# Mixing the first batch once in full width, and wide mixes for the last six pairs, in a Sinkhorn attention and feed-forward kernel

## The chip, the cores and the metric

The kernel runs on one core of a Trainium2 chip. The metric is the device time of one execution in microseconds (us), as the median over repeated runs. The profiler's span is some 1.8 us shorter than the device time. In profiles, PE is TensorE, DVE is VectorE, ACT is ScalarE, POOL is GpSimd, and SP is the engine that issues stores and transposes here. PSUM is the memory in which products land; the kernel takes it in banks of 512 float columns.

Runs of one kernel shift by about 0.5 us (the kernel before, in its first six runs: 245.0 to 245.1 and 245.6).

## The reference, cut to what matters

```
P = exp(sort_net), rows and columns normalised, five times    # (batch, head, 8, 8)
k_sorted = einsum('bhij,bhjcd->bhicd', P, k_blocks)           # 8 blocks of 96 tokens are mixed
v_sorted = einsum('bhij,bhjcd->bhicd', P, v_blocks)
attn     = softmax(scale * q_block @ k_sorted_block.T)        # within each block
x        = (attn @ v_sorted_block), heads side by side        # (3072, 512)
out      = (x @ w_a * (x @ w_b)) @ w_out                      # feed-forward
```

There are 4 batches of 8 heads. The kernel works on pairs of heads: 16 pairs, numbered 0 to 15, four to a batch. "Mix" below means the product with P.

## The kernel before: the parts that count

TensorE (PE) runs one long instruction stream. A batch's feed-forward products (`pf`, `po`) form the bulk, and the next batch's attention units are set between them: `c` (mix), `s` (scores, exp), `o` (weighted sum, then x). The first batch's attention has nothing to hide behind. Its first four blocks (h=0) are done at the start, the other four (h=1) between the first feed-forward products. So its mixes are halved:

```python
def half_mix(h, hp, what, eng, fill=0, cols=512):
    mix = psF.tile([P, 512], FP32, tag="F", name="mixh")      # one bank, four buffers
    keep_busy(mix, fill, cols)                                # filler products
    for c in range(NCH):                                      # 6
        for e in range(2):
            nc.tensor.matmul(..., lhsT=src2[:, e, c*D:(c+1)*D],
                             rhs=s_all[:, 2*hp + e, h*NBH:(h+1)*NBH], ...)   # 64 columns
    copy(eng, ...)                                            # 384 columns
# later pairs
def stage_mix(g, what, engines):
    mix = psA.tile([P, 2, 512], FP32, tag="A", name="mix")    # two banks, two buffers
    for c in range(NCH):
        for e in range(2):                                    # 12 products, half the array wide
            nc.tensor.matmul(mix[e*D:(e+1)*D, c // 3, c % 3 * P:(c % 3 + 1) * P],
                             lhsT=src2[:, e, c*D:(c+1)*D], rhs=s_all[:, 2*g + e], ...)
    ...                                                       # copies to kT or vT
# ... the scores and o_ps use psA too:
sc = psA.tile([P, 2, 512], FP32, tag="A", name="sc")
```

The softmax here doesn't subtract the row's maximum and nothing guards it: scores larger than these inputs give would overflow.

## Time and profile before

The time was 245.06 us at first and 245.04 us beside the changed kernel. PE's stream is the bound, so I cut it at three marks: the column products of P (`pc_ps`), the first feed-forward product after which PE runs without long gaps, and the first query turn of the second batch (`q_ps`). A fourth mark is where the last batch's `pf` begins. I call what lies between **start**, **stretch** and **later stages**.

These are the busy times by stretch of the kernel before. The columns are the window and its length, then busy us of PE, PE's weight loads, DVE, ACT and POOL with instruction counts, the granted clock, the DMA share and GB/s.

```profile
11.70:21.08 9.38, 9.05 (x203) 6.55 (x204) 6.96 (x18) 6.43 (x12) 6.97 (x9) 1.00 1.39 198
21.08:44.87 23.79, 23.69 (x300) 14.87 (x301) 13.13 (x30) 12.98 (x26) 15.02 (x19) 1.00 1.37 200
44.87:193.21 148.34, 148.13 (x1394) 85.30 (x1395) 65.02 (x131) 65.37 (x128) 30.11 (x43) 1.00 0.74 121
```

Read length against PE busy: PE idles 0.33 us in the start, 0.10 in the stretch and 0.21 in all later stages. None of the other four engines is near its limit past the start.

### The profile page before, as it was taken

What the parts mean: (1) busy time and instruction counts of PE and PEld (TensorE: products, weight loads), DVE (VectorE), ACT (ScalarE), POOL (GpSimd) and SP (SyncE); (2) the same over time, 40 slices, a digit from 0 to 9 for tenths busy, and PEclk for the clock granted to TensorE, in tenths of its full rate; (3) what the DMA queues carried; (4) which work ended last, traced back from release to release, by engine and by line L of the source; (5) the groups of instructions that cost most, each with busy time, mean ns of one, the idle gap of its engine ahead of it and who ended that gap; (6) DMA issues with size and microseconds to landing.
All of it is one profiled execution on the core that took longest, in us unless ns stands there. A gap on an engine that the chain in (4) does not pass through costs nothing.

```text
span 243.3 us, 5625 instructions
## 1 busy us (share of the span) xinstructions
PE 237.4 (98%) x2309; PEld 141.6 (58%) x2309; DVE 109.1 (45%) x258; ACT 104.4 (43%) x204; POOL 61.4 (25%) x88
## 2 busy tenths in 40 slices
PE   7999999999999999999999999999999999999994
PEld 7776666666554466666654466666654466665442
DVE  6774557555435234464534144363625144344110
ACT  3675853565630175736330165737330133333001
POOL 8766569623220053240400054200000000000000
PEclk9999999999999999999999999999999999999999
DMA  5999999985999589993964369923524310000132
GB/s 78 202 198 196 196 201 201 203 138 83 158 204 153 130 70 155 171 138 70 136 115 122 115 120 114 159 51 58 47 75 131 109 43 0 3 0 1 46 129 86
DMA packets 53930, 28.04 MB, mean 115 GB/s; under 512 B 30736, under 2 KB 50960, under 8 KB 53904
## 3 DMA queue, kind: packets, MB, share of 16 engines
q0 software_dynamic: 20944, 14.16, 41.6%
q1 hardware_dynamic: 32816, 13.45, 28.0%
q8 instruction: 18, 0.29, 0.5%
q14 instruction: 8, 0.07, 0.1%
q10 hardware_dynamic: 144, 0.07, 0.1%
HBM read 28.32 MB, written 6.29 MB: 142 GB/s over the span
## 4 chain that ended last, share of the span: by engine, by line
PE 93%; DVE 4%; ACT 1%; DMA 1%; issue 0%
PE pf L332 52%; PE po L377 24%; PE mix L281 4%; PE o_ps L231 3%; PE sc L302 2%; PE mixh L180 2%; PE po L362 1%; PE vs_ps L208 1%; PE xt_ps L222 1%; PE sc L195 1%; DMA p_nat<-in_sort_net_dram 1%; PE heat L168 1%; PE two L332 1%; PE q_ps L260 1%; DVE xp L237 1%
## 5 line engine op out<-in xcount | busy, mean ns | idle before, releaser
L353 DVE TENSOR_TENSOR hT<-a_sb,pf 128x384 bf16<-128x384 bf16 x95 | 52.6, 553 | 73.8 <-PE pf L332 46.4
L332 PE MATMUL pf<-xT,w_a_sb 128*128 128x384 bf16 x380 | 78.0, 326 | 0.2 <-ACT xT L162 0.2
L332 PE MATMUL pf<-xT,w_b_sb 128*128 128x384 bf16 x380 | 77.5, 326 | 0.0
L352 ACT CAST a_sb<-pf 128x384 bf16<-128x384 f32 x95 | 45.5, 479 | 60.9 <-PE pf L332 41.3
L377 PE MATMUL po<-w_out_sb,hT 128*128 128x512 bf16 x276 | 61.9, 379 | 0.0
L332 PEld LDWEIGHTS <-w_b_sb 128*128 128x128 bf16 x384 | 37.5, 98 | 24.8 <-issue 0.3
L332 PEld LDWEIGHTS <-w_a_sb 128*128 128x128 bf16 x384 | 34.9, 98 | 22.2
L377 PEld LDWEIGHTS <-hT 128*128 128x128 bf16 x276 | 26.3, 98 | 30.0
L162 ACT COPY o_sb<-po 128x512 f32<-128x512 f32 (+1 forms) x13 | 7.5, 577 | 46.8 <-PE po L377 45.2
L164 DVE COPY o_sb<-po 128x512 f32<-128x512 f32 (+1 forms) x12 | 7.9, 656 | 35.2 <-PE po L377 26.3
L307 ACT ACTIVATE eT<-sc 96x768 bf16<-96x768 f32 x24 | 18.0, 802 | 6.9 <-PE sc L302 6.9
L542 POOL COPY gate<-kT 1x1 bf16<-1x1 bf16 x8 | 1.4, 179 | 74.7 <-ACT kT L162 74.7
L237 DVE TENSOR_TENSOR xp<-o_ps,rec 96x512 bf16<-96x512 f32 x24 | 15.9, 684 | 0.6 <-DVE rec L235 0.2
L162 ACT CAST kT<-mix 128x384 bf16<-128x384 f32 x24 | 10.3, 482 | 8.0 <-PE mix L281 8.0
L95 POOL DMA_DIRECT2D k<-in_k_dram x16 | 11.6, 724 | 4.5 <-PE pf L332 2.3
L95 POOL DMA_DIRECT2D v<-in_v_dram x16 | 11.5, 721 | 3.1 <-DMA w_b_sb<-in_moe_w_b_dram 1.2
L231 PEld LDWEIGHTS <-eT 96*128 96x128 bf16 x256 | 10.4, 97 | 3.2 <-DVE xp L237 0.6
L235 DVE RECIPROCAL rec<-o_ps 96x8 f32<-96x8 f32 x32 | 5.6, 189 | 13.8 <-PE o_ps L231 13.8
L231 PE MATMUL o_ps<-vs,eT 96*128 96x65 bf16 x256 | 11.3, 193 | 0.2 <-DVE xp L237 0.2
L246 POOL COPY qc<-q 128x768 bf16<-128x768 bf16 x10 | 8.4, 842 | 7.2 <-DMA q<-in_q_dram 7.2
L95 POOL DMA_DIRECT2D q<-in_q_dram x12 | 8.7, 721 | 1.7 <-DMA w_a_sb<-in_moe_w_a_dram 0.7
L168 PE MATMUL heat<-warm 128*128 128x128 bf16 x84 | 7.6, 264 | 1.3 <-DVE warm L77 1.3
(80 smaller groups left out, 158.3 us busy)
## 6 DMA issues: line engine op xcount, KB each, us to landing
out_dram<-o_sb SPq DMA_DIRECT2D x17, 256.0 KB, 2.0
k<-in_k_dram POOLq DMA_DIRECT2D x16, 192.0 KB, 6.0
v<-in_v_dram POOLq DMA_DIRECT2D x16, 192.0 KB, 6.4
q<-in_q_dram POOLq DMA_DIRECT2D x12, 192.0 KB, 6.7
w_a_sb<-in_moe_w_a_dram POOLq DMA_DIRECT2D x6, 256.0 KB, 9.8
w_b_sb<-in_moe_w_b_dram POOLq DMA_DIRECT2D x6, 256.0 KB, 10.0
w_out_sb<-in_moe_w_out_dram POOLq DMA_DIRECT2D x3, 512.0 KB, 10.8
out_dram<-o_sb SPq DMA_DIRECT2D x12, 128.0 KB, 2.4
```

The source lines that it names most:

```text
L95: nc.gpsimd.dma_start(out=to, in_=_ap(t, base, [[W, P], [S * D, 2], [1, W]]))
L162: nc.scalar.copy(out=out, in_=in_)
L168: nc.tensor.matmul(ps[:, 0:cols], lhsT=warm[:, 0:P], rhs=warm[:, 0:cols], start=True, stop=True)
L231: nc.tensor.matmul(o_ps[:, e, i * (D + 1):(i + 1) * (D + 1)], lhsT=eT[:, hf, e, i * BLK:i * BLK + P], rhs=vs[0:BLK, i0 + i, V0 - 1 + e * ( ...
L237: nc.vector.tensor_tensor(out=_ap(xp, i0 * 2 * D, [[nxp * 2 * D, BLK], [D, 2], [2 * D, NBH], [1, D]]), in0=_ap(o_ps, 1, [[1024, BLK], [511 ...
L246: nc.gpsimd.tensor_copy(out=qc.rearrange("p c e d -> p e c d"), in_=loaded[g][2].rearrange("p e (c d) -> p e c d", c=NCH))
L281: nc.tensor.matmul(mix[e * D:(e + 1) * D, c // 3, c % 3 * P:(c % 3 + 1) * P], lhsT=src2[:, e, c * D:(c + 1) * D], rhs=s_all[:, 2 * g + e], ...
L307: nc.scalar.activation(out=eT[:, hf, :, 0:HB], in_=sc[0:BLK, :, 0:HB], func=AF.Exp, scale=float(scale))
L332: nc.tensor.matmul(pf[:, 0:HW], lhsT=w_sb[:, kc, m * P:(m + 1) * P], rhs=x_cols(b, kc, t), start=(kc == 0), stop=(kc == KA - 1))
L352: nc.scalar.copy(out=a_sb, in_=pf[:, 0:HW])
L353: nc.vector.tensor_mul(out=hT[:, m, t * HW:(t + 1) * HW], in0=a_sb, in1=ab[1][:, 0:HW])
L377: nc.tensor.matmul(held["po"], lhsT=hTs[b][:, m, c * P:(c + 1) * P], rhs=w_out_sb[:, m, :], start=(m == 0), stop=(m == KO - 1))
```

## The change

The intent was to take work off PE: mix each first-batch pair once, and give the last six pairs a form with 4 products instead of 24. That form gives the mixed tokens on partitions, so they have to be turned by DMA and put in order by POOL. The core of the diff, with cuts:

```diff
-    def half_mix(h, hp, what, eng, fill=0, cols=512):
...
+    def mix_k(g, fill=0):
+        mix = psA.tile([P, 2, 512], FP32, tag="A", name="mix")
+        keep_busy(mix[:, 0], fill)
+        cols = mix.rearrange("p b n -> p (b n)")
+        mix_mms(g, "k", lambda c: cols[:, c * P:(c + 1) * P])     # 12 products of 128 columns
+        nc.scalar.copy(out=..kTs[g % HP].., in_=..mix..)          # 768 columns
+    def mix_v(g):                                   # two one-bank buffers, DVE and ACT copy one each
...
+    def stage_plain(g, what, engines):              # pairs 10 to 15
+        mix = psA.tile([P, 2, 512], FP32, tag="A", name="mix")
+        for e in range(2):
+            nc.tensor.matmul(mix[:, e, 0:W], lhsT=s_all[:, 2 * g + e], rhs=src2[:, e], ...)  # 384 columns
+        ...                                         # copies to nat
+        nc.sync.dma_start_transpose(out=turned, in_=nat...)
+    def in_order(g, what):                          # POOL copies turned to kT or vT
...
-            spread(nc.vector, pc_ps, 0, 2, 0, NBH)  # P of four blocks
-            spread(nc.vector, pc_ps, 2, 6, 0, NBH)
+            to_columns(1)
+            spread(nc.vector, pc_ps, 0, 2)          # P of all eight blocks
+            spread(nc.vector, pc_ps, 2, 2)
+            nc.vector.tensor_copy(out=p_col, in_=pc_ps)
+            spread(nc.gpsimd, p_col, 4, 4)
...
-            us = [lambda: M(0)]                     # second-half mixes between the products
+            us = []
...
-                want = s + 1 if s < slow else -(-(s + 1) * len(units) // (n - spare))
+                want = s if s < slow else -(-(s + 1) * len(units) // (n - spare))
```

The change also has six output buffers (`o_sb`) for three, one `hT` buffer for two, four `kT` and `vT` buffers for three and six buffers for later q loads; pairs 4 to 9 copy their k in one piece of 768 columns. It moves the mixes of pairs 12 and 13 one stage earlier and holds the load of pair 14 back until the third batch's last xT transpose has landed (`gate`).

More of the change, by code (lines that the diff above doesn't have):

```diff
@@ L93, in load_pair @@
                 continue
-            to = ld.tile([P, 2, W], BF16, tag=name, name=name)
+            to = ld.tile([P, 2, W], BF16, tag=name, name=name,
+                         bufs=6 if name == "q2" else None)
             nc.gpsimd.dma_start(out=to, in_=_ap(t, base, [[W, P], [S * D, 2], [1, W]]))
@@ L125 @@
     NBUF = 3
-    kTs = [const.tile([P, S + PAD], BF16, name=f"kT{n}") for n in range(NBUF)]
-    vTs = [const.tile([P, NB, P], BF16, name=f"vT{n}") for n in range(NBUF)]
+    kTs = [const.tile([P, S + PAD], BF16, name=f"kT{n}") for n in range(HP)]
+    vTs = [const.tile([P, NB, P], BF16, name=f"vT{n}") for n in range(HP)]
     eTs = [const.tile([BLK, 2, 2, HB + PAD], BF16, name=f"eT{n}") for n in range(NBUF)]
@@ L131 @@
         nc.vector.memset(t[:, S:], 0.0)
-        nc.vector.memset(t[:, HB:HB + PAD], 0.0)
     for t in vTs:
@@ L169, in keep_busy, with mix_mms @@
                              start=True, stop=True)
-    def half_mix(h, hp, what, eng, fill=0, cols=512):
-        g = h * HP + hp
-        src2 = loaded[hp][0 if what == "k" else 1]
-        to = (kTs if what == "k" else vTs)[g % NBUF]
-        mix = psF.tile([P, 512], FP32, tag="F", name="mixh")
-        keep_busy(mix, fill, cols)
+    def mix_mms(g, what, where):
+        src2 = loaded[g][0 if what == "k" else 1]
         for c in range(NCH):
             for e in range(2):
-                nc.tensor.matmul(
-                    _ap(mix, e * D * 512 + c * CG, [[512, D], [BLK, NBH], [1, CG]]),
-                    lhsT=src2[:, e, c * D:(c + 1) * D],
-                    rhs=s_all[:, 2 * hp + e, h * NBH:(h + 1) * NBH], start=True, stop=True)
-        if what == "k":
-            copy(eng, to[:, 0:HB], mix[:, 0:HB])
-        else:
-            copy(eng, to[:, 0:NBH, 0:BLK], _ap(mix, 0, [[512, P], [BLK, NBH], [1, BLK]]))
+                nc.tensor.matmul(where(c)[e * D:(e + 1) * D], lhsT=src2[:, e, c * D:(c + 1) * D],
+                                 rhs=s_all[:, 2 * g + e], start=True, stop=True)
+    def mix_k(g, fill=0):
[3 more added lines that the diff above has]
+        mix_mms(g, "k", lambda c: cols[:, c * P:(c + 1) * P])
+        nc.scalar.copy(
+            out=_ap(kTs[g % HP], 0, [[S + PAD, P], [CG, NCH], [BLK, NB], [1, CG]]),
+            in_=_ap(mix, 0, [[1024, P], [P, NCH], [CG, NB], [1, CG]]))
+    def mix_v(g):
+        mix = [psF.tile([P, 512], FP32, tag="F", name="mixv") for _ in range(2)]
+        mix_mms(g, "v", lambda c: mix[c // 3][:, c % 3 * P:(c % 3 + 1) * P])
+        for u, eng in enumerate(("dve", "act")):
+            copy(eng, _ap(vTs[g % HP], u * 3 * CG, [[NB * P, P], [CG, 3], [P, NB], [1, CG]]),
+                 _ap(mix[u], 0, [[512, P], [P, 3], [CG, NB], [1, CG]]))
     def half_scores(h, hp):
         g = h * HP + hp
-        kT, qT, eT = kTs[g % NBUF], st[hp, "qT"], eTs[g % NBUF]
+        kT, qT, eT = kTs[hp], st[hp, "qT"], eTs[g % NBUF]
         sc = psA.tile([P, 2, 512], FP32, tag="A", name="sc")
@@ L196, in half_scores @@
                     sc[:, e, i * BLK:(i + 1) * BLK],
-                    lhsT=kT[e * D:(e + 1) * D, i * BLK:i * BLK + P],
+                    lhsT=kT[e * D:(e + 1) * D, (h * NBH + i) * BLK:(h * NBH + i) * BLK + P],
                     rhs=qT[e * D:(e + 1) * D, :, (h * NBH + i) * CG:(h * NBH + i + 1) * CG],
@@ L204, in half_v @@
         g = h * HP + hp
-        vT, vs = vTs[g % NBUF], vss[g % NBUF]
+        vT, vs = vTs[hp], vss[g % NBUF]
         vs_ps = psF.tile([P, NBH, 2, D], BF16, tag="F", name="vs_ps")
         for i in range(NBH):
-            nc.tensor.matmul(vs_ps[:, i], lhsT=vT[:, i], rhs=ident, is_transpose=True)
+            nc.tensor.matmul(vs_ps[:, i], lhsT=vT[:, h * NBH + i], rhs=ident, is_transpose=True)
         nc.vector.tensor_copy(out=vs[0:BLK, 0:NBH, V0:V0 + P],
@@ L267, in turn_v @@
     def turn_v(g):
-        vT, vs = vTs[g % NBUF], vss[g % NBUF]
+        vT, vs = vTs[g % HP], vss[g % NBUF]
         vs_ps = psF.tile([P, NB, P], BF16, tag="F", name="vs_ps")
@@ L272, in turn_v, with stage_v @@
         nc.vector.tensor_copy(out=vs[0:BLK, :, V0:V0 + P], in_=vs_ps[0:BLK])
-    def stage_mix(g, what, engines):
+    def stage_v(g):
+        to = vTs[g % HP]
+        mix = psA.tile([P, 2, 512], FP32, tag="A", name="mix")
+        mix_mms(g, "v", lambda c: mix[:, c // 3, c % 3 * P:(c % 3 + 1) * P])
+        for u, eng in enumerate(("dve", "act")):
+            copy(eng, _ap(to, u * 3 * CG, [[NB * P, P], [CG, 3], [P, NB], [1, CG]]),
+                 _ap(mix, u * 512, [[1024, P], [P, 3], [CG, NB], [1, CG]]))
@@ L275, in stage_mix, with plain @@
+    def plain(g):
+        return g >= 2 * HP + 2
+    def stage_plain(g, what, engines):
         src2 = loaded[g][0 if what == "k" else 1]
-        to = (kTs if what == "k" else vTs)[g % NBUF]
-        pitch, whole = (BLK, S + PAD) if what == "k" else (P, NB * P)
         mix = psA.tile([P, 2, 512], FP32, tag="A", name="mix")
-        for c in range(NCH):
-            for e in range(2):
-                nc.tensor.matmul(
-                    mix[e * D:(e + 1) * D, c // 3, c % 3 * P:(c % 3 + 1) * P],
-                    lhsT=src2[:, e, c * D:(c + 1) * D],
-                    rhs=s_all[:, 2 * g + e], start=True, stop=True)
@@ L285, in stage_mix @@
-        for hf, eng in enumerate(engines):
-            n = 2 // len(engines)
-            for u in range(n):
-                d1 = _ap(to, (hf + u) * 3 * CG, [[whole, P], [CG, 3], [pitch, NB], [1, CG]])
-                s1 = _ap(mix, (hf + u) * 512, [[1024, P], [P, 3], [CG, NB], [1, CG]])
-                copy(eng, d1, s1)
-        if what == "v" and g > HP:
-            nc.sync.dma_start_transpose(out=vss[g % NBUF][:, :, V0:V0 + P],
-                                        in_=to.rearrange("p i t -> p (i t)"))
+        for e in range(2):
+            nc.tensor.matmul(mix[:, e, 0:W], lhsT=s_all[:, 2 * g + e], rhs=src2[:, e],
+                             start=True, stop=True)
@@ new lines, in stage_plain @@
+        nat = att.tile([P, NCH, 2, D], BF16, tag="nat", name="nat")
+        step = 2 // len(engines)
+        for u, eng in enumerate(engines):
+            copy(eng, nat[:, :, u * step:(u + 1) * step].rearrange("p c e d -> p e c d"),
+                 mix[:, u * step:(u + 1) * step, 0:W].rearrange("p e (c d) -> p e c d", c=NCH))
+        turned = att.tile([P, NCH, P], BF16, tag="turned", name="turned")
+        nc.sync.dma_start_transpose(out=turned, in_=nat.rearrange("p c e d -> p (c e d)"))
@@ new lines, in stage_plain, with return_v @@
+        st[g, what] = turned
+    def in_order(g, what):
+        if what == "k":
+            to = kTs[g % HP][:, 0:S].rearrange("p (i c t) -> p c i t", i=NB, c=NCH)
+        else:
+            to = vTs[g % HP][:, :, 0:BLK].rearrange("p i (c t) -> p c i t", c=NCH)
+        nc.gpsimd.tensor_copy(out=to, in_=st[g, what].rearrange("p c (i t) -> p c i t", i=NB))
+    def return_v(g):
+        nc.sync.dma_start_transpose(out=vss[g % NBUF][:, :, V0:V0 + P],
+                                    in_=vTs[g % HP].rearrange("p i t -> p (i t)"))
@@ L295, in stage_scores @@
     def stage_scores(g):
-        kT, qT, eT = kTs[g % NBUF], st[g, "qT"], eTs[g % NBUF]
+        kT, qT, eT = kTs[g % HP], st[g, "qT"], eTs[g % NBUF]
         for hf in range(2):
@@ L336, in hT_of @@
         if b not in hTs:
-            hTs[b] = ffp.tile([P, KO, S], BF16, tag="hT", name="hT")
+            hTs[b] = ffp.tile([P, KO, S], BF16, tag="hT", name="hT", bufs=1)
         return hTs[b]
@@ L363, in ffn_last @@
                                  rhs=w_out_sb[:, m, n0:n1], start=(m == 0), stop=(m == KO - 1))
-            o_sb = ffp.tile([P, 512], FP32, tag="o_sb", name="o_sb", bufs=3)
+            o_sb = ffp.tile([P, 512], FP32, tag="o_sb", name="o_sb", bufs=6)
             copy(eng, o_sb[:, 0:n1 - n0], po[:, 0:n1 - n0])
@@ L384, in store @@
     def store(b, c, po):
-        o_sb = ffp.tile([P, DMODEL], FP32, tag="o_sb", name="o_sb", bufs=3)
+        o_sb = ffp.tile([P, DMODEL], FP32, tag="o_sb", name="o_sb", bufs=6)
         copy("act" if c % 2 == 0 else "dve", o_sb, po)
@@ L404 @@
             p_rep = const.tile([BH, NB * NB, CG // 2], FP32, name="p_rep")
+            heat = psA.tile([P, 2, 512], FP32, tag="A", name="heat")
             pc_ps = psA.tile([P, NB, BH], FP32, tag="A", name="pc_ps")
-            heat = psA.tile([P, 2, 512], FP32, tag="A", name="heat")
             keep_busy(heat[:, 0], 32, P)
@@ L456 @@
             to_columns(0)
-            spread(nc.vector, pc_ps, 0, 2, 0, NBH)
-            spread(nc.vector, pc_ps, 2, 6, 0, NBH)
+            to_columns(1)
[3 more added lines that the diff above has]
+            spread(nc.gpsimd, p_col, 4, 4)
             load_ab(2)
             load_ab(3)
-            half_mix(0, 0, "k", "act", fill=2, cols=256)
-            half_mix(0, 0, "v", "dve")
-            to_columns(1)
-            half_mix(0, 1, "k", "act")
-            nc.vector.tensor_copy(out=p_col, in_=pc_ps)
-            spread(nc.gpsimd, p_col, 0, 8, NBH, NBH)
+            mix_k(0, fill=1)
+            mix_v(0)
+            mix_k(1)
             half_scores(0, 0)
             half_v(0, 0)
-            half_mix(0, 1, "v", "dve")
-            half_mix(0, 2, "k", "act", fill=1)
+            mix_v(1)
+            mix_k(2, fill=1)
             half_o(0, 0)
@@ L474 @@
             half_v(0, 1)
-            half_mix(0, 2, "v", "act")
-            half_mix(0, 3, "k", "act", fill=1)
+            mix_v(2)
             half_x(0, 0, "dve")
+            mix_k(3, fill=1)
             half_o(0, 1)
@@ L480 @@
             half_v(0, 2)
-            half_mix(0, 3, "v", "act", fill=1)
+            mix_v(3)
             half_x(0, 1, "dve")
@@ L513, in units_half @@
         def units_half():
-            def M(hp):
-                half_mix(1, hp, "k", "act")
-                half_mix(1, hp, "v", "act")
             def R(hp):
@@ L520, in R @@
                 half_v(1, hp)
-            us = [lambda: M(0)]
+            us = []
             for hp in range(HP):
-                if hp + 1 < HP:
-                    us.append(lambda hp=hp: M(hp + 1))
                 us.append(lambda hp=hp: R(hp))
@@ L531, in units_half, with c_ @@
             return us
-        def units_full(b):
-            g0, us = b * HP, []
-            def c_(g):
-                if g < 2 * HP - 2:
-                    turn_q(g)
-                stage_mix(g, "k", ("act",))
-                stage_mix(g, "v", ("dve", "act"))
-                if 2 * HP - 2 <= g < B * HP - 2:
-                    nc.gpsimd.tensor_copy(out=gate, in_=kTs[g % NBUF][0:1, 0:1])
-                    load_pair((g + 2) // HP, (g + 2) % HP)
-            def s_(g):
-                stage_scores(g)
-                if g == HP:
-                    turn_v(g)
-                if g in (HP, HP + 1):
-                    stage_q(g + 2)
-                if 2 * HP <= g + 1 < B * HP:
-                    pair_q(g + 1)
-                    stage_q(g + 1)
-            def o_(g):
-                stage_o(g)
-                to_xT(g)
-            for u, n in ((c_, 0), (s_, 0), (c_, 1), (s_, 1), (c_, 2), (o_, 0), (s_, 2), (c_, 3),
-                         (o_, 1), (s_, 3), (o_, 2), (o_, 3)):
-                us.append(lambda u=u, g=g0 + n: u(g))
-            return us
+        def c_(g):
+            if g < 2 * HP - 2:
+                turn_q(g)
+            if plain(g):
+                stage_plain(g, "k", ("act",))
+                stage_plain(g, "v", ("dve", "act"))
+            else:
+                mix_k(g)
+                stage_v(g)
+            if plain(g):
+                pair_q(g)
+                stage_q(g)
+            else:
+                if g > HP:
+                    return_v(g)
+                if g >= 2 * HP - 2:
+                    nc.gpsimd.tensor_copy(out=gate, in_=kTs[g % HP][0:1, 0:1])
+                    load_later(g)
@@ new lines, in s_, with o_, load_later, plan @@
+        def s_(g):
+            stage_scores(g)
+            if g == HP:
+                turn_v(g)
+            if g in (HP, HP + 1):
+                stage_q(g + 2)
+            if 2 * HP <= g + 1 < B * HP and not plain(g + 1):
+                pair_q(g + 1)
+                stage_q(g + 1)
+        def o_(g):
+            stage_o(g)
+            to_xT(g)
+        def load_later(g):
+            if g < B * HP - 2:
+                load_pair((g + 2) // HP, (g + 2) % HP)
+        seq = []
+        def plan(b, *names):
+            for name in names:
+                seq.append((b, {"c": c_, "s": s_, "o": o_}[name[0]], int(name[1:])))
@@ new lines @@
+        plan(0, "c4", "s4", "c5", "s5", "c6", "o4", "s6", "c7", "o5", "s7", "o6", "o7")
+        plan(1, "c8", "s8", "c9", "s9", "c10", "o8", "c11", "o9", "s10", "c12", "s11", "o10", "o11",
+             "c13")
+        plan(2, "s12", "c14", "s13", "o12", "c15", "s14", "o13", "s15", "o14", "o15")
+        after = [[] for _ in seq]
+        for n, (b, u, g) in enumerate(seq):
+            if u is c_ and plain(g):
+                late = 3 if g % HP == 0 else 2
+                after[n + 1] += [lambda g=g, what=what: in_order(g, what) for what in "kv"]
+                if late == 3:
+                    after[n + 3].append(lambda g=g: nc.gpsimd.tensor_copy(
+                        out=gate, in_=xT_of(g // HP - 1)[0:1, HP - 1, 0:1]))
+                after[n + 2 * late - 3].append(lambda g=g: load_later(g))
+                after[n + late].append(lambda g=g: return_v(g))
@@ L564, in interleave, with unit @@
+        def unit(u, g, then):
+            u(g)
+            for f in then:
+                f()
+        units = [[] for _ in range(B)]
+        for (b, u, g), then in zip(seq, after):
+            units[b].append(lambda u=u, g=g, then=then: unit(u, g, then))
         def interleave(steps, units, spare, slow=0):
@@ L571, in interleave, with paced @@
                     done += 1
-        def paced(ab, po, units, spare):
+        def paced(ab, po, units, spare, last):
             steps = ab + po
             total = len(steps) - 2 * spare
-            done = 0
+            main, done = len(units) - last, 0
             for now, step in enumerate(steps, 1):
                 step()
-                while done < len(units) and done * total < now * len(units):
+                while done < main and done * total < now * main:
                     units[done]()
                     done += 1
+                if now == len(steps) - 1 and last:
+                    units[main]()
         steps = [lambda: ffn_ab(0, 0, 0, begun[0:2]), lambda: ffn_ab(0, 1, 0, begun[2:4]),
@@ L591 @@
             po = [f for c in range(NCH) for f in ffn_out(b, c)]
-            paced(ab, po, units_full(b + 1) if b + 1 < B else [], 3 if b == 0 else 2)
+            paced(ab, po, units[b], 3 if b == 0 else 2, 1 if b == 1 else 0)
 _INS = ['q', 'k', 'v', 'sort_net', 'moe_w_a', 'moe_w_b', 'moe_w_out']
```

## The prediction

> **What bounds the kernel now.** I read the first page's busy shares, then the chain that ended last, then the chain in order of time, and last the timelines of single engines around the start.
>
> ```profile
> PE 237.4 (98%) x2309; PEld 141.6 (58%) x2309; DVE 109.1 (45%) x258; ACT 104.4 (43%) x204; POOL 61.4 (25%) x88
> PE 93%; DVE 4%; ACT 1%; DMA 1%; issue 0%
> L281 PE MATMUL mix<-s_all,k 128*64 128x128 bf16 x144 | 6.3, 222 | 0.0
> L180 PE MATMUL mixh<-s_all,k 128*64 128x64 bf16 x96 | 3.0, 199 | 0.1
> ```
>
> PE is busy 98% of 243.3 us and makes 93% of the chain; granted clock is full in all slices. DVE and ACT are under half. So past the start, time changes only by what PE's instruction stream gains or loses, or by a new PE wait. The mean durations of these rows (222 ns, 199 ns) are latencies of pipelined instructions and overlap; what an instruction costs the stream is the distance between starts, and I take that from the chain:
>
> ```profile
> 84.17 1.30 PE pf L332 x8
> 85.47 0.79 PE mix L281 x24
> 86.26 2.71 PE pf L332 x16
> ...
> 106.17 0.49 PE o_ps L231 x16
> 106.66 3.90 PE pf L332 x24
> ```
>
> Eight 384-column products take 1.30 us, 162.5 ns each. The 24 mixing products of one pair (k and v) take 0.79, and the 16 products after them 2.71 where 16 x 162.5 ns is 2.60: leaving the mix costs 0.11 more. After o_ps the 24 products cost 3.90, exactly 24 x 162.5, so this loss comes with the half-width mix and not with any change of work. A pair's mix costs 0.90 us of stream.
>
> The exception is the start, to about 21 us, where engines hand work to each other in short turns:
>
> ```profile
> 13.34 0.34 PE L195 MATMUL sc<-qT,kT 64*128 64x96 bf16 x8
> 15.24 0.34 PE L195 MATMUL sc<-qT,kT 64*128 64x96 bf16 x8
> 17.31 0.34 PE L195 MATMUL sc<-qT,kT 64*128 64x96 bf16 x8
> 19.08 0.34 PE L195 MATMUL sc<-qT,kT 64*128 64x96 bf16 x8
> 21.08 0.32 PE L332 MATMUL pf<-xT,w_a_sb 128*128 128x384 bf16 x1 [0.18 <-ACT xT L162]
> ```
>
> These are the score products of the first four pairs, some 1.9 us apart, and the point from which PE runs without gaps.
>
> **What the Trainium skill says.** "TensorE: Matmul & The Clock Gate", section "Back-to-back issue gap", gives N/2.4 + 2.5 ns for the warm isolated gap: 162.5 ns at 384 columns, exactly what this trace has. Its sustained figures for streams with weight loads (131 ns at 512) do not fit: 12 po products take 2.60 to 2.71 us here, about 216 ns each. "ScalarE: Activation LUTs", section "What ACT_TABLE_LOAD costs", gives 186 + 0.833 N ns for an ACTIVATE, with some 93 ns of overlap back to back: 506 and 826 ns at 384 and 768; the trace has 479 and 800, and two back-to-back 768 copies take 1.50 together, an overlap of 0.10. "TensorEngine Tiling (Array Packing)", section "PSUM Bottleneck", warns that after tiling the eviction can become the limit; at the start of the changed kernel I expect just that. No page that I found gives the 0.11 us around tiled products.
>
> **The change, part by part.**
>
> (1) *Wide mixes for the last six pairs.* Now 2 products of 384 columns for k and 2 for v, with the 128x128 mixing matrix as weights: 4 x 162.5 = 0.65 us in place of 0.90. Six pairs: 6 x 0.25 = **1.5 us off PE**. Evictions keep their size (k: one of 768 for two of 384 on ACT, 0.80 for 0.96). Added: 12 DMA transposes, 12 POOL copies of 128x768 (the like-sized qc copy is 842 ns, 10 us of POOL in all, and POOL is 75% free). All this hangs on latency: eviction 0.9, transpose 3 to 6 (medians 2.8, 4.6, 5.8), two POOL copies 1.7, for v another transpose 5.8: some 15 us. In the new order the scores of pair 10 come four units after its mix, each 2.5 steps of over 1.3 us, and those of 14 and 15 further in time: hidden. The tightest spot is pair 14, whose load now waits for the last xT of the third batch: 12 to 13 us after that unit (DVE 1.8, transpose 2.8, issue 0.7 and 1.4, landing 6 to 6.4) against 14.2 us of PE work (10 steps of 1.3, a wide mix, a score unit). It should just fit.
>
> (2) *First batch's second-half mixes gone* from the stretch 21 to 45 us: four groups of 24 narrow products, 0.38 to 0.50 us each in the chain (1.9), plus about 0.11 after three of them: 2.2 us of PE. But they hid latency. Walk from 23.36 us, where the last two xT-dependent products start. Without mixes the first score unit comes after step 1 and needs the two-bank PSUM buffer of a gate product, which DVE frees after: a_sb at +0.37 to 0.85 (ACT 0.48), product 0.55 to 1.40, second product 0.55 to 1.95. So scores start at +1.97, where PE is ready at +0.65. Then step 2 and the o unit end at +3.85, step 3 at +5.15; before, this point plus two mixes was at +5.11. Nothing of the first two is gained. After step 3 the new pacing puts scores, an xT transpose and o_ps in one lump (units 3 to 5 of 12 at once): o_ps must wait for a 0.81 us exp, a stall of about 0.45. The third mix pays for that with about 0.2 over, the fourth is gained whole, 0.6. **About 0.8 off.**
>
> (3) *The start.* More work there, not only moved. To_columns twice before the first spread: 0.2. First spread 128x256 (between 289 ns for 128 and 547 for 384: about 418) for 128x128: 0.13. First mix at 12.66, not 12.34. Then full mixes: 12 products at 28 ns and about 0.05, so 0.36 for 0.31. The larger matter is ACT and the PSUM ring: ACT copies k in 768 columns (0.80, 0.70 back to back) for 384 (0.48, 0.38), and half of each v: per pair 0.70 + 0.38 + exp 0.70 back to back. And k's mix now shares the two two-bank buffers with scores and o_ps, so scores of pair n wait until ACT has copied the k of pair n+1. The walk: kT0 ready 13.94, scores 0 at 13.98 (+0.64); ACT goes v0 14.32, k1 15.02, exp0 15.73, v1 16.11; the POOL spread for pairs 2 and 3 can start only after the weight issue at 13.87, so 14.61 to 15.72, mix k2 15.77 to 16.2, copied 17.05: scores 1 at 17.1 (+1.9). PE then does vs 0.33, v2 0.36, x 0.29, fill 0.25, k3 0.36 to 19.0, copy to 19.85: scores 2 at 19.9 (+2.6). Exp2 to 21.1, o2, scores 3 at 21.5 (+2.4), exp3 to 22.65, o3, xT copy: gapless stream from about 23.3 in place of 21.08. **About 2.25 us added.**
>
> (4) *Rest.* Six o_sb buffers take away DVE's one wait of 4.5 us on a store; the chain crosses DVE there for 72.50 to 74.63 but PE loses only about 0.2 us in that whole stage (38.99 busy of 39.2). **0.2 off.** One hT buffer costs nothing: its first writer follows the last reader in PE order.
>
> Sum: +2.25 - 0.8 - 1.5 - 0.2 = -0.25 us. So 2.5 us of gain, nearly all handed back at the start. As the order seems tuned for this version, I lean a little further down than the sum: **244.4 us**.
>
> **Rivals.** *The start costs little*: if PE's filler products and gaps absorb the longer copies, only the first 0.3 to 0.8 remains, and the time is 242.5 to 243. For it: ACT is idle 1.0 us before its first copy. Against: the scores' buffer wait in my walk has no slack from pair 1 on. *The interleaved stretch gains all of its 2.2 us*: about 243. Against: DVE's second product frees the buffer that the first scores need. *A transfer becomes the bound*: pair 14's load or a transpose queued on SP comes late and PE waits 1 to 3 us: 246 to 247. For it: 12 more transposes, in-order SP; against: DMA is at 20 to 60% there, and six store buffers loosen SP. *POOL becomes the bound*: its copies plus issues still leave it half idle; only latency counts. I give it little.
>
> **Range and chances.** Start 2.25 give or take 0.9, stretch 0.8 give or take 0.7, mixes 1.5 give or take 0.3, a late transfer at one in six. 8 in 10: 242.4 to 246.2. A gain over 2% needs under 240.2, more than all the removed PE work (1.5 + 2.2 + 0.2 = 3.9) allows with any loss at the start; a loss over 2% needs 250.
>
> **What would show it.** Right: PE's four score groups of the start at about 14.0, 17.1, 19.9 and 21.5, with ACT nearly unbroken and its k copies of 128x768 near 800 ns; gapless PE from 23 us; one or two PE waits between 25 and 32 us on DVE's hT and on the exp; wide mixes at 0.65 us with the 24 products after them at 3.90. Wrong: PE gapless by 21.5 us; or waits over 0.5 us on a POOL copy, a DMA or a transpose after 84 us; or wide mixes near 0.8.

## The result, and the profile after

The changed kernel took 245.21 us (245.06 to 245.67, six runs) beside 245.04 us. The ratio is 1.0003, 95% interval 0.9988 to 1.0017: the same. Here and below a ratio is the mean time of one kernel's runs over that of the kernel before in the same rounds, so it is not quite the ratio of the medians. Executions over 1.5% slower than the fastest of the same kernel are left out of the means.

The first page after, busy shares and chain:

```profile
PE 233.6 (96%) x2081; PEld 138.7 (57%) x2091; DVE 110.2 (45%) x259; ACT 102.4 (42%) x186; POOL 70.4 (29%) x97
PE 89%; DVE 3%; ACT 3%; DMA 2%; issue 1%; POOLq 0%; DVEq 0%; ACTq 0%
```

PE is 3.8 us less busy in a span of the same length, though part of that is ten `po` products missing from this trace (266 of 276 in their row). By stretch, columns as before:

```profile
11.66:23.51 11.85, 10.08 (x201) 7.36 (x202) 7.88 (x20) 8.39 (x14) 8.76 (x12) 1.00 1.40 198
23.51:46.55 23.04, 21.44 (x204) 13.11 (x205) 13.29 (x30) 9.71 (x18) 14.40 (x19) 1.00 1.35 197
46.55:193.40 146.85, 146.22 (x1266) 83.91 (x1275) 64.92 (x131) 64.62 (x116) 38.23 (x51) 1.00 0.88 136
```

The start is 2.47 us longer: PE has 1.03 more to do and idles 1.77 for 0.33. The stretch lost 2.25 us of PE work and is only 0.75 shorter, because its idle time rose from 0.10 to 1.60. The later stages are 1.49 shorter. Together that is +0.23 us; the last batch took 0.19 less in this run (49.90 for 50.09), so the two spans are equal.

PE's score groups in the start, and where PE's gapless run begins (start, duration, then the wait in brackets):

```profile
13.97 0.34 PE L201 MATMUL sc<-qT,kT 64*128 64x96 bf16 x8
16.87 0.35 PE L201 MATMUL sc<-qT,kT 64*128 64x96 bf16 x8 [0.54 <-ACT kT L184]
19.84 0.35 PE L201 MATMUL sc<-qT,kT 64*128 64x96 bf16 x8 [0.54 <-ACT kT L184]
21.44 0.34 PE L201 MATMUL sc<-qT,kT 64*128 64x96 bf16 x8
23.51 0.32 PE L354 MATMUL pf<-xT,w_a_sb 128*128 128x384 bf16 x1 [0.18 <-ACT xT L162]
```

The two waits on ACT's k copies are new. PE's list of waits has two more that the kernel before did not have (us in total, times, longest):

```profile
PE sc L201 <- DVE hT L375: 1.1, 1, 1.1
PE o_ps L237 <- ACT eT L206: 0.5, 1, 0.5
```

Both fall in the stretch, at 27.74 and 32.02 us: there PE now waits where it used to mix. A wide mix (`mix` by L295) in the chain of the later stages:

```profile
99.04 2.71 PE pf L354 x16
101.75 0.65 PE mix L295 x4
102.40 3.90 PE pf L354 x24
```

It takes 0.65 us, and the 24 products after it 3.90: the 0.11 after a half-width mix (2.71 for 16 products instead of 2.60, see the prediction) is gone.

### The profile page after: what moved, and what is told of

Read it like the earlier page. It is cut to its first block, busy times and chain, and to the rows that moved or that the text cites. A ratio compares the mean times of both kernels' runs of the same rounds, so it can differ in the third digit from the quotient of the medians.

```text
span 243.3 us, 5181 instructions
## 1 busy us (share of the span) xinstructions
PE 233.6 (96%) x2081; PEld 138.7 (57%) x2091; DVE 110.2 (45%) x259; ACT 102.4 (42%) x186; POOL 70.4 (29%) x97
## 4 chain that ended last, share of the span: by engine, by line
PE 89%; DVE 3%; ACT 3%; DMA 2%; issue 1%; POOLq 0%; DVEq 0%; ACTq 0%
PE pf L354 51%; PE po L399 24%; PE o_ps L237 3%; PE sc L324 2%; PE mix L176 2%; DMA q_first<-in_q_dram 2%; PE mix L295 2%; ACT kT L184 1%; PE po L384 1%; PE sc L201 1%; PE vs_ps L214 1%; ACT eT L206 1%; PE xt_ps L228 1%; PE q_ps L266 1%; DVE xp L243 1%
## 5 line engine op out<-in xcount | busy, mean ns | idle before, releaser
L399 PE MATMUL po<-w_out_sb,hT 128*128 128x512 bf16 x266 | 61.0, 379 | 0.5
L311 POOL COPY kT<-turned 128x768 bf16<-128x768 bf16 x6 | 5.0, 828 | 34.3 <-DMA turned<-nat 27.4
L565 POOL COPY gate<-kT 1x1 bf16<-1x1 bf16 x4 | 0.7, 178 | 34.3 <-ACT kT L184 34.3
L184 ACT CAST kT<-mix 128x768 bf16<-128x768 f32 x10 | 8.0, 800 | 5.6 <-PE mix L176 5.6
L162 ACT CAST nat<-mix 128x768 bf16<-128x768 f32 (+1 forms) x12 | 7.7, 638 | 4.2 <-PE mix L295 3.5
```

What stands on the lines that cost most here:

```text
L162: nc.scalar.copy(out=out, in_=in_)
L184: nc.scalar.copy(out=_ap(kTs[g % HP], 0, [[S + PAD, P], [CG, NCH], [BLK, NB], [1, CG]]), in_=_ap(mix, 0, [[1024, P], [P, NCH], [CG, NB], [ ...
L399: nc.tensor.matmul(held["po"], lhsT=hTs[b][:, m, c * P:(c + 1) * P], rhs=w_out_sb[:, m, :], start=(m == 0), stop=(m == KO - 1))
```

## The experiments

The kernels are numbered; number 5 was built and not run. The theory: three separate effects cancel, namely a longer start, a stretch whose gain turned into waits, and wide mixes that keep their full gain. The rivals: the parts are worth nothing each; the start is held by ACT's volume of work and not by a buffer; the stretch is held by work and not by order. All times are medians of the fast runs.

| kernel | start | stretch | later stages | time | ratio to before |
|---|---|---|---|---|---|
| before | 9.38 | 23.79 | 148.34 | 245.04 | 1 |
| changed | 11.85 | 23.04 | 146.85 | 245.21 | 1.0003 |
| 1 old first batch, wide mixes | 9.37 | 23.79 | 146.97 | 244.25 | 0.9953 |
| 2 new first batch, no wide mixes | 11.84 | 23.04 | 148.35 | 247.2 | 1.0078 |
| 3 k in one-bank buffers | 11.10 | 23.05 | 146.85 | 244.3 | 0.9963 |
| 4 even pacing | 11.83 | 21.39 | 146.85 | 243.35 | 0.9924 |
| 6 k split, two-bank buffer | 12.80 | 23.04 | 146.85 | 246.04 | 1.0029 |
| 7 k split, one-bank buffers | 11.21 | 23.05 | 146.85 | 244.48 | 0.9969 |
| 8 = 7 with 4 | 11.21 | 21.39 | 146.85 | 242.77 | 0.9896 |
| 9 = 8, eight wide pairs | 11.20 | 21.39 | 146.60 | 242.57 | 0.989 |
| 10 = 7 without filler | 10.94 | 23.04 | 146.85 | 244.08 | 0.9956 |
| 11 three output buffers | 13.11 | 23.04 | 147.12 | 245.52 | 1.0018 |
| 12 = 9, load not gated | 11.21 | 21.38 | 146.36 | 242.9 | 0.9917 |
| 13 all together | 10.56 | 21.39 | 147.14 | 242.82 | 0.9899 |

Start, stretch and later stages come from each kernel's one profiled run, between the marks named above. They repeat within 0.02 us where nothing that bears on them was edited, with three exceptions: the start of kernel 11 and the later stages of kernels 11 and 13, discussed there, and kernel 1's later stages (0.12 over the changed kernel). These 0.12 arise at one score unit at 97.5 us, whose weight load waited 0.43 us for a query transpose; kernel 11 has its 0.2 us wait at the same unit.

### 1 and 2: one part alone

Kernel 1 takes the changed kernel and puts `half_mix`, the old start and the old second-half units back:

```diff
-            mix_k(0, fill=1)
-            mix_v(0)
+            half_mix(0, 0, "k", "act", fill=2, cols=256)
+            half_mix(0, 0, "v", "dve")
...
-            us = []
+            us = [lambda: M(0)]
```

> The changed kernel with the first batch mixed in halves again, as before; the wide mixes of the last six pairs stay. Theory (the two parts simply add: wide mixes take 1.5 us off PE's stream, the new first batch gives 1.7 back): PE without gaps from about 21.1 us again, four narrow mix groups back between 23 and 34 us, time 1.5 us under the kernel before: 243.5, ratio 0.994. Rival (the wide mixes cost something elsewhere, or something else of the change such as the single hT buffer or six store buffers carries the balance): 244.5 to 245.2.

Measured: 244.25 us (243.57 to 244.73), ratio 0.9953 (0.9937 to 0.997). Start and stretch are those of the kernel before to 0.01 us, and the later stages 1.37 shorter. The theory's 0.994 lies at the interval's lower edge; no gain at all is excluded.

Kernel 2 keeps the new first batch and drops the wide mixes (the old order of the later units comes back with them; its lines are cut here):

```diff
-        return g >= 2 * HP + 2
+        return False
```

> The changed kernel without the wide mixes: all later pairs mixed in 24 half-width products and in the old order of units; the first batch stays in full width. Theory: 1.5 us over the changed kernel, 246.7, ratio to before 1.007; each pair's mix back at 0.79 us and the products after it 0.11 longer. Rival (the wide mixes were worth nothing, and the first batch cost nothing): 245.2.

Measured: 247.2 us (246.87 to 247.55), ratio 1.0078 (1.0063 to 1.0092). The half-width mix and the products after it stand in its chain as before:

```profile
141.63 0.79 PE mix L176 x24
142.42 2.71 PE pf L354 x16
```

Its start (11.84) and stretch (23.04) are those of the changed kernel, its later stages (148.35) those of the kernel before. So by the stretches the wide mixes give about 1.5 us and the new first batch costs about 1.7. The small change of time is two opposite ones, not two nothings. The rest of the change, which kernel 2 still has (buffers of `o_sb`, `hT`, `kT` and q), moves the later stages by 0.01 us.

### 3, 6 and 7: what holds the start

Kernel 3 puts the first batch's k mixes into two one-bank buffers, both copied by ACT. The scores' two-bank ring then has no k mix in it, and ACT has more work:

```diff
+    def mix_k0(g, fill=0):
+        mix = [psF.tile([P, 512], FP32, tag="F", name="mixk") for _ in range(2)]
...
+        for u in range(2):
+            copy("act", ..kTs[g % HP].., ..mix[u]..)
```

> The changed kernel with the first batch's k mixed into two one-bank buffers of the other pool, both copied by ACT (two copies of 384 columns for one of 768: 0.16 us more of ACT per pair). Theory A (the scores wait because k's mix sits in the same two-bank ring, so scores of pair n wait for the copy of k of pair n+1): the two waits of scores on ACT's kT, 0.54 us each, and the late start of scores 1 are gone, PE without gaps from about 22.0 in place of 23.5 us, time 243.5 to 244.2. Rival B (ACT's volume of work in the start is the limit): ACT has more work, so no gain, 245.2 to 245.6.

Measured: 244.3 us (244.25 to 244.89), ratio 0.9963 (0.9949 to 0.9978). Its score groups:

```profile
14.12 0.34 PE L209 MATMUL sc<-qT,kT 64*128 64x96 bf16 x8
16.31 0.34 PE L209 MATMUL sc<-qT,kT 64*128 64x96 bf16 x8
18.84 0.34 PE L209 MATMUL sc<-qT,kT 64*128 64x96 bf16 x8
20.59 0.34 PE L209 MATMUL sc<-qT,kT 64*128 64x96 bf16 x8
```

Both waits on ACT's k copies are gone, though ACT does slightly more (8.46 us of the start for 8.39). So the ring made them and not ACT's volume. But the start is only 0.75 us shorter where I had expected 1.5. What remained?

Kernel 6 keeps the ring and lets ACT and DVE copy one bank of k each:

```diff
+        mix = psA.tile([P, 2, 512], FP32, tag="A", name="mix")
...
+        for u, eng in enumerate(("act", "dve")):
+            copy(eng, ..kTs[g % HP].., ..mix, bank u..)
```

> The changed kernel, first batch's k still in the two-bank ring, but a bank each copied by ACT (384 columns) and DVE (384). ACT has about 0.3 us less per pair and the copy that scores wait for is 0.25 us shorter. The one-bank run gave 0.75 us of the start's 2.4 back and showed ACT unbroken from 12.9 to 17.5 us. Theory AB (both the ring and ACT's volume hold the start): scores at about 13.8, 16.35, 18.9, 20.5, PE without gaps about 0.9 us earlier, 244.3. Theory A alone (ring wait, ACT volume irrelevant): only the shorter copy counts where PE waited, 0.25 twice, 244.7.

Measured: 246.04 us (245.97 to 246.67), ratio 1.0029 (1.0017 to 1.0042). It is slower, against both theories. ACT's and DVE's first k copies:

```profile
13.71 0.48 ACT L162 CAST kT<-mix 128x384 bf16<-128x384 f32 x1 [1.49 <-PE mix L176]
14.22 0.56 DVE L164 CAST kT<-mix 128x384 bf16<-128x384 f32 x1 [0.46 <-ACT kT L162]
```

DVE began only when ACT had ended and is shown waiting for it. The two copies ran one after the other, 1.07 us in place of 0.80, and PE's waits for the k copy rose to 0.41, 0.81 and 0.81 us. So this run did not shorten the copy as planned. By lengthening it, it confirmed that the scores wait for it.

Kernel 7 is kernel 3 with one buffer copied by ACT and one by DVE:

```diff
-        for u in range(2):
-            copy("act", ..
+        for u, eng in enumerate(("act", "dve")):
+            copy(eng, ..
```

> Both edits: k in two one-bank buffers, one copied by ACT and one by DVE. Theory AB: what is left of the start's loss is the later first mix (0.3 us) and PE's longer mixes, PE without gaps from about 21.9 in place of 23.5, 1.6 us under the changed kernel: 243.6. Rival C (the late POOL spread for pairs 2 and 3 is the third limit): second scores not before 16.1 and only 1.0 to 1.2 us gained, 244.1. Rival D (DVE becomes the limit, as it takes 0.55 us more per pair): no gain over the one-bank run, 244.3.

Its copies do run together:

```profile
13.31 0.48 ACT L162 CAST kT<-mixk 128x384 bf16<-128x384 f32 x1 [1.22 <-PE mixk L176]
13.48 0.56 DVE L164 CAST kT<-mixk 128x384 bf16<-128x384 f32 x1
```

Measured: 244.48 us (244.28 to 245.02), ratio 0.9969 (0.9956 to 0.9983), the same as kernel 3. The 243.6 of theory AB did not come. ACT is busy 7.49 us of the start for 8.46 in kernel 3, and it bought nothing; with the ring gone, ACT's volume is not the limit. (Rival D, that DVE becomes the limit, would give the same time; kernel 10 speaks against it.)

### 10: the rest of the start

Kernel 7's PE shows only short waits in the start, none over 0.23 us: it is busy 10.40 us of 11.21, where the kernel before has 9.05 of 9.38. That looks like PE's own line. Kernel 10 takes two filler products out of kernel 7:

```diff
-            mix_k0(2, fill=1)
+            mix_k0(2)
...
-            mix_k0(3, fill=1)
+            mix_k0(3)
```

> The run with k in two one-bank buffers, split over ACT and DVE, but without the two filler products ahead of the k mixes of pairs 2 and 3. That run still started its gapless stretch 11.2 us after the column products, before 9.4, although PE waited for nobody in its list. Theory E (what is left of the start's loss is PE's own longer mixes, in line with everything else on PE): each filler takes 0.3 us of that line, so scores 2 and 3 and the gapless stretch come 0.5 to 0.6 us earlier, and the time is 243.9. Rival F (latency from engine to engine sets the pace and the filler only fills): no change, 244.5; or slower if the granted clock falls.

Measured: 244.08 us (243.99 to 244.82), ratio 0.9956 (0.994 to 0.9972), and a start 0.27 us shorter. The second filler counted: scores of pair 2 stand 6.92 us after the column products, 7.21 in kernel 7. The first did not: without it PE waits 0.28 us for the P of pairs 2 and 3 that POOL spreads.

```profile
15.34 0.53 PE L176 MATMUL mixk<-s_all,k 128*64 128x128 bf16 x12 [0.28 <-POOL s_all L154]
```

So after the ring is out of the way, the line of PE instructions sets the pace at pair 2, and POOL's spread stands just behind it. That PE's line is longer because of the wider mixes is the plain reading: a k mix holds PE 0.46 us from start to start ahead of `o_ps` (18.41 to 18.87 in kernel 7), and 0.31 before (14.58 to 14.89). Eight mixes at 0.15 more would be 1.2 us, an estimate, beside the 1.35 by which PE is busier in kernel 7. No run takes the width alone away, so this part is read and not tested.

### 4, 8: the stretch

Kernel 4 sets the second-half units one by one:

```diff
-        interleave(steps, units_half(), 1, 3)
+        interleave(steps, units_half(), (0, 0, 1, 2, 3, 5, 6, 8, 9, 11, 12, 12))
```

(with `want = wanted[s]`, the number of units done after each step).

> The changed kernel with the units of the second half of the first batch spread one by one: first scores after step 2 in place of step 1, and each o_ps at least one step after its scores. Theory (the missing mixes had hidden latency; PE now waits 1.13 us on DVE's hT and 0.46 on ACT's exp): both waits gone, about 1.4 us off, 243.8. Rival (the stretch is limited by the work of ACT or DVE there, so the wait only moves): 244.8 to 245.2, with PE waits in other places between 26 and 45 us.

Measured: 243.35 us (243.34 to 243.87), ratio 0.9924 (0.9911 to 0.9937). Its stretch, columns as above:

```profile
24.01:45.40 21.39, 21.26 (x204) 13.16 (x205) 13.10 (x30) 9.74 (x18) 13.93 (x18) 1.00 1.36 200
```

PE idles 0.13 us for 1.60, and neither of the two waits is in its list any more. Not one instruction was removed. The stretch's loss was order alone.

Kernel 8 joins kernels 7 and 4.

> The start of the run before and the even pacing of the second-half units together. If the two losses are separate, their gains add: 1.6 (or 1.1) and 1.65 to 1.9, so 241.8 to 242.3, ratio to before 0.987 to 0.989. If they overlap (a faster start only makes PE reach the same ACT and DVE waits sooner), 243.0 to 243.4.

Measured: 242.77 us (242.67 to 242.83, four runs), ratio 0.9896 (0.9882 to 0.9909). The start is that of 7, the stretch that of 4: the two losses are separate and the gains add.

### 11: the store buffers

Only the two `bufs=6` of `o_sb` go back to 3.

> The changed kernel with three output buffers as before, six in the change. The prediction gave the six buffers 0.2 us; the traces show the second stage at 39.30 us in both kernels. Expected: no change, 245.2, stage 39.30. If the six buffers do carry something that another cost of the change hides: 245.4 or more, and DVE waits of some us on a store again.

Measured: 245.52 us (245.14 to 246.97), ratio 1.0018 (0.9996 to 1.0041), no difference that can be told. From the first query turn to the second batch's first `pf` the profiled run has 39.30 us, as before and after the change. It was the run with 246.97 us: POOL's spread came late behind a weight issue and PE waited 1.0 us for it, most of the 1.26 us that its start is longer. The later stages' 0.27 hold a wait of 0.2 us on a query transpose. I take neither for an effect of the buffers, but one profile can't show that. The DVE wait on a store that the expectation looked for did not come back with three buffers.

### 9, 12 and 13: how far the wide mixes go

Kernel 9 makes pairs 8 and 9 wide too, on top of kernel 8 (the order of the third batch's units changes with it):

```diff
-        return g >= 2 * HP + 2
+        return g >= 2 * HP
-        plan(0, ... "c7", "o5", "s7", "o6", "o7")
+        plan(0, ... "c7", "o5", "c8", "s7", "o6", "o7", "c9")
```

> As the run before, with the wide mixes for pairs 8 and 9 too (eight pairs), whose mixes move into the second batch's stage. If each wide mix is worth 0.25 us wherever it stands: 0.5 us under the run before, about 241.5. If the latency of the longer way (transpose, POOL copies, transpose) or the load gated behind the second batch's last xT shows here: PE waits in front of the scores or mixes of pairs 8 to 10 between 85 and 100 us, and 242 to 244.

Measured: 242.57 us (242.51 to 242.87, four runs), ratio 0.989 (0.9876 to 0.9904). Half of the 0.5 us came. The chain passes through the load of pair 10, which the new order holds behind the second batch's last xT:

```profile
83.78 6.00 DMA v<-in_v_dram
89.77 0.05 issue
89.82 0.50 PE mix L303 x2
```

Kernel 12 lets that load go early:

```diff
-                late = 3 if g % HP == 0 else 2
+                late = 3 if g == 3 * HP else 2
```

> The run with eight wide pairs, but the load of pair 10 no longer held back until the second batch's last xT has landed. In that run the mix of pair 10 waited for its v, loaded 6.0 us before, and eight wide mixes gained 0.25 us over six where 0.5 was expected. Theory: with the earlier load the wait is gone and the other 0.25 us appear: 242.3, second to fourth stage 146.35 us from the first query turn to the last batch. Rival: the load only collides with the transposes elsewhere, no change or slower.

The profiled run did as expected (later stages 146.36, 242.42 us), but the others spread up to 244.35; median 242.9, ratio 0.9917 (0.9892 to 0.9942). Kernel 9 has a range of 0.36 us, this one 1.93.

Kernel 13 puts all together: kernel 12 without filler, and POOL's spread one weight issue earlier:

```diff
             spread(nc.gpsimd, p_col, 4, 4)
+            load_ab(1, (1,))          # was issued ahead of the spread
```

> All that helped, together: k in two one-bank buffers split over ACT and DVE, no filler ahead of the k mixes of pairs 2 and 3, even pacing, eight wide pairs with the load of pair 10 early; and the POOL spread for pairs 2 and 3 issued ahead of a weight load that it stood behind (the run without filler waited 0.28 us for it). From the six-pair run with pacing (242.77): 0.5 for the two more wide pairs, 0.3 for the one filler that counted, 0.3 for the earlier spread: 241.7, ratio 0.985. From column products to the gapless stretch 10.6 us, then 21.4 to the first query turn of the second batch, then 146.35. If the weight chunk that now comes later is missed: a PE wait on it near 26 to 28 us and no gain over 242.4.

Measured: 242.82 us (241.81 to 243.71), ratio 0.9899 (0.9876 to 0.9922). Start (10.56) and stretch (21.39) came as expected; the later stages did not. PE's list of waits, and SP's issue of the second batch's last xT transpose:

```profile
PE pf L362 <- DMA xT<-xp: 0.6, 1, 0.6
79.24 3.45 SPq L348 DMA_TRANSPOSE xT<-xp  x1
```

With the load of pair 10 under way from 75 us on, that issue took 3.45 us where the shortest in the same run took 1.21, and the transpose landed 6.45 us after its issue began. In kernel 9, with the gate, two such issues took 2.61 together. So in the median the gate paid for itself (242.57 for 242.9 us), though the intervals of kernels 9 and 12 overlap and kernel 12's fastest run is the faster one. The same collision is the likely cause of kernel 12's spread, which I did not trace run by run. Of the versions run, kernel 9 has the lowest median and a narrow range; kernel 8 is 0.2 us above it, with an interval that overlaps. Kernel 13's start and stretch with kernel 9's gate would be the next thing to try; it was not run.

## Why the prediction was right or wrong

Right in outline was the reason: a PE gain, 2.24 us by the marks where some 2.5 were stated, handed back at the start. The measured 245.21 lies in the range, 0.8 above the stated 244.4. By its own steps:

- **Wide mixes, 1.5 us off.** Measured 1.49 between the marks, and 1.50 in kernel 2. The size rested on two things read from the chain, the 0.79 and the 0.11 behind it; both are gone after (0.65, then 3.90). Six eviction, transpose, copy and transpose chains were hidden, as stated, although the new transposes landed after a median of 6.2 us rather than 3 to 6. The tight spot at pair 14 held, too: PE waited for no load there.
- **Stretch, 2.2 us of work, 0.8 gained.** Measured 2.25 and 0.75. Both named waits appeared, 1.13 us on DVE's product and 0.46 on the exp (stated: about 1.3 and 0.45). Kernel 4 shows that they were the loss.
- **Start, 2.25 us added.** Measured 2.47. The score groups came at 13.97, 16.87, 19.84 and 21.44 where 13.98, 17.1, 19.9 and 21.5 were stated. The ring was real: kernel 3 removes it, and the two waits go. But the text called "ACT and the PSUM ring" the larger matter, and one matter. The two were not one: kernel 3 gains with more work on ACT, and kernel 7 gains nothing with less. Nor was the ring the larger part: 1.7 of the 2.47 us stay without it (11.10 for 9.38), most of them in PE's own longer line (busy 10.41 for 9.05), which kernel 10 shortened. The walk had a mix at 0.36 us for 0.31; it is 0.46 where an untiled group follows. It also put POOL's spread on the path of the second scores (over at 15.72, then the mix of k2 at 15.77). The spread came 0.42 us earlier than that, and PE reached this mix through its own line:

```profile
14.19 1.11 POOL L154 TENSOR_TENSOR s_all<-mask,p_col 128x512 bf16<-128x512 bf16 x1
15.46 0.53 PE L176 MATMUL mix<-s_all,k 128*64 128x128 bf16 x12
```

So the two errors, too long a wait for POOL and too short a mix, went opposite ways. That the score times agree so closely is in part luck.

- **Output buffers, 0.2 off.** This step failed: the stage has 39.30 us in both kernels. DVE's wait of 4.5 us was not in that stage either, and the store can hardly have held it. The copy in question starts at 193.30 us, and after the change, with six buffers, the same copy is idle just as long, now put down to PE:

```profile
193.30 0.69 DVE L164 COPY o_sb<-po 128x512 f32<-128x512 f32 x1 [4.49 <-DMA out_dram<-o_sb]
193.44 0.69 DVE L164 COPY o_sb<-po 128x512 f32<-128x512 f32 x1 [4.49 <-PE po L399]
```

The profile names the releaser that came last; here two seem to have come close together. In kernel 2, with six buffers, the store is named again.

- **The lean.** The sum was -0.25, and 244.4 was put 0.4 below that because the order "seems tuned for this version". It was not: kernel 4 gained 1.65 us of the stretch by order alone. Without this lean the stated time would have been 244.8.

The rivals: "the start costs little" is refuted by its 2.47 us, and "the stretch gains all" by the 1.60 us of idle time. "POOL becomes the bound" did not happen in the changed kernel: PE's list has no wait on POOL. It came close: PE waits for POOL's spread 0.28 us in kernel 10 and 1.0 in the profiled run of kernel 11. "A transfer becomes the bound" did not happen in the changed kernel, and did for 0.6 us in kernel 13, where a load was set beside the xT transposes.

## What to carry to other kernels

When PE is the bound, count what a removed instruction group was hiding before booking its time as gain: here 2.25 us of work left a stretch and 1.5 us of waits came in its place, until the units were spread anew. A buffer pool shared by two kinds of work ties them together; ask what the next user of that buffer waits for. And price a half-width group with the loss that follows it, not by its own length.

## What the Trainium skill lacked or had wrong

- "TensorEngine Tiling (Array Packing)" and "TensorE: Matmul & The Clock Gate", Part 3, give no cost for going between half-width and full-width products; the first page says, under "Key Properties", that a change of tiling mode drains TensorE, which agrees with the loss seen here but has no figure. Here the products after a half-width mix took 0.11 us longer (2.71 for 2.60), and after a full-width one they did not (3.90 for 24). The "PSUM Bottleneck" section's warning that evictions can become the limit held only through a shared buffer: taking 0.97 us of copying off ACT in the start (kernel 7 against 3) changed nothing.
- "TensorE: Matmul & The Clock Gate", "Back-to-back issue gap": the sustained 131 ns at 512 columns does not appear in this stream of weight loads and products; the isolated 216 ns does (12 in 2.60 to 2.71 us), and at 384 columns 162.5 ns.
- "DMA: Bandwidth & Descriptors", "DMA Transpose (X-bar)", has constraints and no durations; the rates and the one duration that other places of the skill give are not from issue to landing and not for these shapes. Here DMA transposes landed after medians of 3.0 (xT), 4.4 (queries), 4.6 (v) and 6.2 us (the new ones) in the changed kernel, and beside a load one xT issue took 3.45 us for 1.21.
- "PSUM — Partial Sum Buffer" quotes that ScalarE and VectorE can access PSUM in parallel as long as there is no bank collision; no run here speaks against it. In kernel 6, copies from two banks of one buffer ran one after the other (0.48, then 0.56 us); from two buffers they ran together. The trace shows a wait of the one on the other, so this is likely the program's ordering within one buffer and not the memory.
